# Build-time order of a three-stage attention and gating kernel: VectorE and GpSimd pieces kept apart, TensorE lengths as measured, all choices drawn anew

## The chip, the cores and the metric

One core of one Trainium2 chip runs the kernel. The metric is the device time of one execution in microseconds (us). The profile is one execution, recorded by the hardware profiler. PE is TensorE, DVE is VectorE, ACT is ScalarE, POOL is GpSimd, SP is SyncE, whose queue issues every DMA here.

## The reference

Three stages follow one another for 4 batches (B) of 576 tokens (S), everything in float32:

```python
# 1: attention, 8 heads of 64; tokens in fours (mean), and a band of +-3 tokens
out = repeat(softmax(q_d @ k_d.T / 8) @ v_d, 4) + softmax(band(q @ k.T / 8)) @ v
# 2: 4 experts on x = out (512 channels), each a causal attention of width 64; the 2 best logits of x @ w_gate
x2 = sum over the 2 chosen e of w_e * (softmax(causal(x@wq[e] @ (x@wk[e]).T / 8)) @ (x@wv[e]) @ wo[e])
# 3: gated tail: a causal convolution of 5 taps per channel
y = (sigmoid(conv5(x2)) * (x2 @ w_val)) @ w_out
```

`w_val` and `w_out` arrive as float64 and are rounded to float32 on the chip from their two words. Products of stages 2 and 3 are made of three products of float32r halves (high by high, high by low, low by high), so every operand of them is split once into a high part (ACT) and a low part (a subtraction on DVE or POOL, L499).

## The kernel before, in words

The kernel does not loop over its work in a fixed order. It describes pieces. `@piece(engine, cost, reads, writes)` gives a piece its engine, an estimated length, its buffers and, through `plan.due`, a due time. `Plan.order` is a list scheduler that runs while the kernel is built: whenever an engine is free in its model, it gives that engine the piece due first among those whose inputs are done and for whose buffers there is room. The program is then written in that order, and on the chip each engine runs its list strictly in order, held only by semaphores. Due times are priorities and not clock times.

`PARAMS` holds 336 numbers and names: due times and lengths of the stages (`f`/`fl` attention, `p`/`pl` projections, `e`/`el` experts, `t`/`tl` tail, one per batch; `wq` the weights of q, k, v and gate, `wt`/`wl` those of the tail), how many PSUM banks or buffers a kind may hold (`c_`, `r_`), the engine of single steps (`q_`, `k_`, `v_` the sums of fours at L651 to L685, `n_` the band's normalising at L734, `xl_`, `gl_` the low parts at L499, `w_` the experts' normalising at L1021, `ve_`, `xe_`, `mp_`, `pt_`, `qe_` copies out of PSUM at L489), how many of the 5 taps ACT takes (`cv_`; it multiplies at L1129 and POOL adds at L1133; the other taps are one DVE instruction each at L1138), and in which form a band softmax is done (`a_`).

A batch goes through attention in 4 pairs of heads (scores L745 and L787, maxima L699, their scaling L704, exponentials L709, sums L726 to L730, values L813, sum of both paths L821). Then come projections in 3 products each (L848 to L850), experts by 64 queries (scores again L848 to L850, minima L988, exponentials L997, normalising L1021, transposes L1029, values L1068) and the tail in two halves of 256 and 320 tokens. The result of attention stands in 4 pairs of buffers `xh`, `xl`, which the projections of the same batch free again. A float64 chunk takes DVE steps L526 to L550, ACT steps and three POOL instructions (L558 to L560); it uses the one `v4` buffer and four of the `o` buffers.

The costs that the planner counts with:

```python
def f32r(n):
    return max(0.417 * n, 107) / 1000 + 0.002
def gps(n, k=1):
    return 0.15 * k + 0.0021 * n + 0.102 * (k - 1)
```

It knows nothing of DVE and POOL holding each other up.

Of the kernel before, what the change touches and what calls it, by code (L numbers as in the profile page):

```python
# [21 lines left out]
TINY64 = 2.0 ** -15 * 1.125      # the float whose bits are the upper word of a float64 2^-126  # L22
# [14 lines left out]
    "k_30": "pool", "k_31": "dve", "k_32": "dve", "k_33": "pool", "late": 1.5, "mp_00": "act", "mp_01": "act",  # L37
# [30 lines left out]
    "w_315": "pool", "w_316": "pool", "w_317": "dve", "w_318": "pool", "wl": 88.75, "wl_o": "pool",  # L68
    "wl_out": "dve", "wl_qk": "dve", "wl_vg": "dve", "wq": 71.47, "wt": 39.26, "xe_00": "dve", "xe_01": "dve",
# [7 lines left out]
}  # L77

# [1 line left out]
# The kernel below describes pieces of work: an engine, a rough length, the buffers that are read and  # L80
# written, and when the piece is due. Plan puts them in an order that keeps the engines busy with the
# buffers there are; the program is then written in that order.

class Buf:
    """one use of a slot of a pool"""
# [10 lines left out]
class Piece:  # L96
    def __init__(self, engine, cost, delay, due, fn):
        self.engine, self.cost, self.delay, self.due, self.fn = engine, cost, delay, due, fn
        self.after, self.before, self.bufs, self.needs = set(), [], [], []
        self.ready = 0.0  # L100


class Plan:
    # until the result can be used: by another engine, by the same one
# [15 lines left out]
    def piece(self, engine, cost, reads=(), writes=(), delay=None, after=()):  # L120
        """a piece waits for the writers of what it reads; what it reads and writes, it has to itself"""
        def add(fn):
            p = Piece(engine, cost, self.DELAY[engine] if delay is None else (delay, delay), (self.due, len(self.pieces)), fn)
# [17 lines left out]
            p.after.discard(p)  # L141
            self.pieces.append(p)
            return p
        return add

    def order(self):
        """list scheduling: an engine that is free takes the piece due first of those that can start"""
        free = {k: list(range(len(v))) for k, v in self.pools.items()}
        used = dict.fromkeys(self.caps, 0)
        turn = dict.fromkeys(self.fifo, 0)  # L150
        waiting = {}
        queues = {e: [] for e in self.DELAY}
        for p in self.pieces:
# [24 lines left out]
        while True:  # L178
            for e, queue in queues.items():
# [3 lines left out]
                for i, (_, p) in enumerate(queue):  # L183
                    if room(p):
                        break
# [75 lines left out]
def gps(n, k=1):  # L261
    return 0.15 * k + 0.0021 * n + 0.102 * (k - 1)
# [976 lines left out]
```

## Time and profile before

| | before |
|---|---|
| three runs | 455.19, 456.3, 458.0 us; median 456.3 |
| span of the profiled execution, first to last instruction | 454.2 us |
| busy: PE, DVE, ACT, POOL | 401.4, 383.5, 261.4, 207.6 us |
| moved over the DMA queues | 36.39 MB |

The page gives only the span of the profiled execution; it lies 2.1 us under the median of the runs. A busy PE is one with a product on its way: the records of neighbouring products overlap, so full PE busy time is not PE at its peak.

### The profile page before, as it was taken

To read this page: it belongs to the slowest core of one execution; us is meant where nothing else is said; L and a number is where in the kernel's file an instruction comes from. 1 tells how busy PE (TensorE), PEld (TensorE's weight loads), DVE (VectorE), ACT (ScalarE), POOL (GpSimd) and SP (SyncE) were. 2 spreads that over 40 slices of the span, in tenths; PEclk is the share of its full clock that TensorE was granted. 3 is DMA by queue.
4 is the path that set the end of the run, shared out by engine and by line. 5 is a ranking of instruction groups with operands and counts; after the bars stand their busy time and mean duration, and the time that the engine had idled before them with its cause. 6 is when DMAs were issued, how large, how long until landed. Compare 5 with 4: busy or idle time off the path is not lost.

```text
span 454.2 us, 11162 instructions
## 1 busy us (share of the span) xinstructions
PE 401.4 (88%) x3984; PEld 352.5 (78%) x3984; DVE 383.5 (84%) x1083; ACT 261.4 (58%) x844; POOL 207.6 (46%) x347
## 2 busy tenths in 40 slices
PE   3678688889789578988999899999999999999997
PEld 3467576867568468877977789989887999888996
DVE  6878998698998999669789987697899787979695
ACT  7374655347577666434757754544775534757551
POOL 6355667446663764545454632322342603455100
PEclk9997899999999899999999999999999999999999
DMA  7988665522233111131613040020222000000102
GB/s 179 252 194 222 170 172 134 150 78 75 56 81 100 46 48 48 52 100 30 190 33 107 1 140 13 17 67 30 82 57 57 5 1 0 25 25 2 58 26 79
DMA packets 29078, 36.39 MB, mean 80 GB/s; under 512 B 3424, under 2 KB 18784, under 8 KB 29024
## 3 DMA queue, kind: packets, MB, share of 16 engines
q1 hardware_dynamic: 29024, 35.69, 27.9%
q8 instruction: 31, 0.51, 0.5%
q14 instruction: 23, 0.19, 0.1%
HBM read 30.96 MB, written 4.72 MB: 79 GB/s over the span
## 4 chain that ended last, share of the span: by engine, by line
PE 49%; DVE 33%; DMA 8%; issue 5%; POOL 2%; ACT 1%; SPq 1%; DVEq 0%; POOLq 0%; ACTq 0%
PE ps L848 12%; PE ps L849 10%; PE ps L850 10%; DMA v<-in_vx_dram 5%; DVE row L1138 4%; PE ps L1068 4%; PE ps L1029 3%; PE ps L813 3%; DVE mx L699 2%; DVE pe L1021 2%; DVE mmin L988 2%; PE ps L799 2%; DVE sm L726 2%; PE ps L745 1%; DMA vw<-in_vx_dram 1%
## 5 line engine op out<-in xcount | busy, mean ns | idle before, releaser
L1138 DVE SCALAR_TENSOR_TENSOR row<-row,cw,row 128x256 f32<-128x256 f32 (+1 forms) x96 | 60.2, 638 | 4.0 <-POOL row L1133 2.9
L997 ACT ACTIVATE pe<-ps,mmin 128x64 f32<-128x64 f32 (+4 forms) x80 | 40.0, 502 | 20.4 <-PE ps L1029 8.6
L1029 PE MATMUL ps<-ident,pe 128*128 128x128 f32 x192 | 33.6, 284 | 13.4 <-ACT pe L997 4.6
L1021 POOL TENSOR_SCALAR pe<-pe,es,ew 128x128 f32<-128x128 f32 (+8 forms) x39 | 25.4, 652 | 42.2 <-DVE es L1014 24.7
L709 ACT ACTIVATE p<-ps,mx 128x64 f32<-128x64 f32 (+1 forms) x104 | 34.4, 347 | 16.6 <-DVE mx L704 11.4
L848 PE MATMUL ps<-xh,wqk_h 128*128 128x320 f32 (+1 forms) x128 | 40.2, 314 | 1.4 <-DVE qla L962 0.6
L848 PE MATMUL ps<-gh,wout_h 128*128 128x256 f32 (+1 forms) x128 | 40.4, 316 | 0.0
L988 DVE TENSOR_REDUCE mmin<-ps 128x1 f32<-128x64 f32 (+4 forms) x80 | 35.4, 447 | 5.6 <-PE ps L984 5.0
L849 PE MATMUL ps<-gl,wout_h 128*128 128x256 f32 (+1 forms) x128 | 37.8, 296 | 0.0
L850 PE MATMUL ps<-xh,wqk_l 128*128 128x320 f32 (+1 forms) x128 | 37.8, 295 | 0.0
L849 PE MATMUL ps<-xl,wqk_h 128*128 128x320 f32 (+1 forms) x128 | 37.7, 295 | 0.0
L850 PE MATMUL ps<-gh,wout_l 128*128 128x256 f32 (+1 forms) x128 | 37.7, 295 | 0.0
L787 PE MATMUL ps<-kz,qz 128*64 128x64 f32 x640 | 29.2, 240 | 8.6 <-POOL kz L412 6.5
L1029 PEld LDWEIGHTS ps<-ident,pe 128*128 128x128 f32 x192 | 21.8, 141 | 18.0 <-ACT pe L997 5.0
L1133 POOL TENSOR_TENSOR row<-row,row 128x256 f32<-128x256 f32 (+1 forms) x32 | 26.4, 826 | 20.1 <-ACT row L1129 18.7
L787 PEld LDWEIGHTS ps<-kz,qz 128*64 128x64 f32 x640 | 24.4, 150 | 14.1 <-POOL kz L412 7.0
L1068 PE MATMUL ps<-mpT,vE 128*64 128x256 f32 (+3 forms) x352 | 28.3, 296 | 1.6 <-DVE row L1150 0.9
L499 POOL TENSOR_TENSOR xl<-row,xh 128x348 fp32r<-128x348 f32 (+1 forms) x21 | 17.6, 850 | 26.3 <-ACT xh L495 26.3
L813 PEld LDWEIGHTS ps<-pT,vw 128*64 128x64 f32 x640 | 22.9, 150 | 6.7 <-issue 2.7
L699 DVE TENSOR_REDUCE mx<-ps 128x6 f32<-128x384 f32 (+2 forms) x48 | 24.6, 516 | 3.9 <-PE ps L787 2.7
L813 PE MATMUL ps<-pT,vw 128*64 128x58 f32 (+1 forms) x640 | 26.0, 238 | 2.1 <-ACT p L709 1.3
L499 POOL TENSOR_TENSOR gl<-row,gh 128x320 fp32r<-128x320 f32 (+1 forms) x20 | 18.0, 904 | 20.2 <-ACT gh L495 20.2
(187 smaller groups left out, 1420.2 us busy)
## 6 DMA issues: line engine op xcount, KB each, us to landing
vw<-in_vx_dram SPq DMA_DIRECT2D x32, 160.0 KB
qz<-in_qT_dram SPq DMA_DIRECT2D x32, 144.0 KB
kt<-in_kT_dram SPq DMA_DIRECT2D x16, 288.0 KB
kz<-in_kT_dram SPq DMA_DIRECT2D x32, 144.0 KB
v<-in_vx_dram SPq DMA_DIRECT2D x16, 288.0 KB
out_dram<-o SPq DMA_DIRECT2D x16, 160.0 KB
v<-in_w_val_dram SPq DMA_DIRECT2D x4, 512.0 KB
v<-in_w_out_dram SPq DMA_DIRECT2D x4, 512.0 KB
```

The costliest lines, as they stand in the source:

```text
L499: (nc.vector if eng == "dve" else nc.gpsimd).tensor_sub(lo(), src(), hi().bitcast(F32))
L787: nc.tensor.matmul(s.t[64 * h:64 * h + 64, (w - w0) * 64:(w - w0) * 64 + 64], qb.t[:, h, WQ * w:WQ * w + 64], kz.t[:, h, WQ * w:WQ * w + 6 ...
L813: nc.tensor.matmul(po.t[64 * h:64 * h + 64, q0 - t0:q1 - t0], vw.t[:, w, 64 * h:64 * h + 64], pT.t[:, (w - w0) // 2, 64 * h:64 * h + q1 - ...
L848: nc.tensor.matmul(p, ah, bh, start=first, stop=False)
L849: nc.tensor.matmul(p, ah, bl, start=False, stop=False)
L850: nc.tensor.matmul(p, al, bh, start=False, stop=last)
L988: nc.vector.tensor_reduce(out=m.t[:, a:a + 1], in_=s.t[:, :c1 - c0], op=ALU.min, axis=AX.X)
L997: nc.scalar.activation(pe.t[:, c0:c1], s.t[:, :c1 - c0], AF.Exp, bias=m.t[:, 0:1], scale=-1.0, accum_out=es.t[:, a:a + 1])
L1021: ENG[en].tensor_scalar(pe.t[:, :N], pe.t[:, :N], es.t[:, 0:1], ew.t[:, i % 2, t, pr:pr + 1], op0=ALU.mult, op1=ALU.mult)
L1029: nc.tensor.transpose(pt.t[:, (nf - 1 - j) * P:(nf - j) * P], pe.t[:, j * P:(j + 1) * P], ident)
L1068: nc.tensor.matmul(av.t[64 * e:64 * e + 64, z:n], vE.t[:kr, j, 2 * pr + e, :], pT.t[:kr, e, k0:k0 + (n - z) // 64, :].rearrange("p k q -> ...
L1138: nc.vector.scalar_tensor_tensor(g.t[:, :nn], x2.t[:, k:k + nn], cw.t[:, m, k:k + 1], g.t[:, :nn], op0=ALU.mult, op1=ALU.add)
```

## The change

The planner gets a kind for each piece. DVE and POOL pieces that work in SBUF alone get the kind "port"; TensorE pieces of half-height tiles get "half".

```diff
 class Plan:
-    # until the result can be used: by another engine, by the same one
+
+    PATIENCE, AHEAD, HEAD = 0.1, 4.0, {"dve": 0.13, "pool": 0.05}
...
-                for i, (_, p) in enumerate(queue):
+                other = {"dve": "pool", "pool": "dve"}.get(e)
+                i = None
+                for j, (_, p) in enumerate(queue):
                     if room(p):
-                        break
-                else:
+                        if i is None:
+                            i = j
+
+                        if p.kind != "port" or port[other] <= now + self.PATIENCE:
+                            i = j
+                            break
+                        if p.due[0] > queue[i][1].due[0] + self.AHEAD:
+                            break
+                if i is None:
                     continue
+                p = queue[i][1]
...
+                if p.kind == "port":
+                    cost = max(cost, port[other] - now + cost - min(cost, self.HEAD[e]))
+                    port[e] = now + cost
                 if e == "pe":
-                    # the array runs at half its rate after a beat with much idling
+                    if p.kind != groups:
+                        cost += 0.09 if p.kind else 0.14
+                        groups = p.kind
...
-def f32r(n):                     # one float32r product
-    return max(0.417 * n, 107) / 1000 + 0.002
...
+def f32r(n):
+    return max(0.459 * n, 112) / 1000
...
-    return 0.15 * k + 0.0021 * n + 0.102 * (k - 1)
+    return 0.19 * k + 0.0021 * n + 0.08 * (k - 1)
```

A port piece is passed over while a port piece of the other engine runs on for more than 0.1 us, if another piece that can start is due at most 4 us later; otherwise it is placed anyway, with the wait added to its length. A few more lengths change by some hundredths of a microsecond.

No instruction's arithmetic changes, nor the number of TensorE products. `PARAMS` is drawn anew: of the choices of engine 9 of 16 change for `v_`, 7 of 16 for `k_`, 5 of 16 for `q_`, 17 of 32 for `n_`, 16 of 32 for `xl_`, 34 of 72 for `w_`, 4 of 8 for `gl_`. The count of band parts with a scaled maximum (`a_` 1) goes from 11 to 18 of 32. Taps on ACT: `cv_00` 2 to 4, `cv_01` 2 to 1, `cv_10` 2 to 1, `cv_11` 2 to 4, `cv_20` 3 to 4, `cv_21` 3 to 1, `cv_30` 1 to 2, `cv_31` stays 1. To ACT go `ve_0`, `ve_1`, `mp_20`, `mp_31`, `xe_01`, `xe_20`, `pt_3`, `qe_31`; to DVE go `pt_1`, `qe_10`, `qe_20`, `qe_21`; `wl_qk` goes from DVE to POOL. Due times: `wq` 71.47 to 251.21, `wt` 39.26 to 27.09, `f1` 34.43 to 31.69 with `fl1` 21.4 to 87.16, `p0` 60.17 to 103.9, `e2` 196.82 to 68.9 with `el2` 42.86 to 204.57, and all others.

## Rows read from the trace of the kernel before

**Rows 1.** The page, busy us, share of the span and instructions of each engine.
```profile
PE 401.4 (88%) x3984; PEld 352.5 (78%) x3984; DVE 383.5 (84%) x1083; ACT 261.4 (58%) x844; POOL 207.6 (46%) x347
```
**Rows 2.** Stretches: us, busy PE, PEld, DVE, ACT, POOL, granted clock, DMA share, GB/s.
```profile
0.00:40.00 40.00, 26.19 (x276) 21.72 (x278) 31.02 (x86) 23.98 (x81) 20.71 (x48) 0.92 0.86 205
40.00:180.00 140.00, 112.37 (x1193) 92.42 (x1190) 129.07 (x349) 86.06 (x289) 85.24 (x119) 0.97 0.36 104
180.00:260.00 80.00, 72.93 (x736) 64.95 (x737) 66.75 (x191) 46.94 (x153) 40.12 (x64) 1.00 0.25 73
260.00:440.00 180.00, 179.04 (x1715) 163.07 (x1712) 148.06 (x441) 101.05 (x316) 61.50 (x118) 1.00 0.12 37
440.00:454.20 14.20, 10.87 (x77) 10.33 (x75) 8.64 (x20) 3.37 (x8) 0.00 (x0) 0.98 0.21 77
```
**Rows 3.** The page, the chain that ended last, share of the span by engine.
```profile
PE 49%; DVE 33%; DMA 8%; issue 5%; POOL 2%; ACT 1%; SPq 1%; DVEq 0%; POOLq 0%; ACTq 0%
```
**Rows 4.** Waits of PE between 260 and 440 us, the longest: us, times, longest.
```profile
PE ps L848 <- DVE qla L962: 0.6, 1, 0.6
```
**Rows 5.** Waits of all engines between 40 and 180 us: us, times, longest.
```profile
ACT p L709 <- DVE mx L704: 9.8, 7, 2.3
...
PE ps L1029 <- ACT pe L997: 4.6, 1, 4.6
```
**Rows 6.** Groups of DVE between 40 and 180 us: busy us, mean ns, idle before.
```profile
L1138 DVE SCALAR_TENSOR_TENSOR row<-row,cw,row 128x256 f32<-128x256 f32 x12 | 10.6, 882 | 0.1
...
L1021 DVE TENSOR_SCALAR pe<-pe,es,ew 128x384 f32<-128x384 f32 (+6 forms) x9 | 6.7, 748 | 0.1
L726 DVE TENSOR_SCALAR sm<-sm 128x4 f32<-128x4 f32 (+2 forms) x22 | 6.4, 298 | 0.1
...
L704 DVE TENSOR_SCALAR mx<-mx 112x3 f32<-112x3 f32 (+2 forms) x12 | 5.9, 493 | 0.1
```
**Rows 7.** The same lines over the span: ns min/median/max, first and last start us.
```profile
L1138 DVE SCALAR_TENSOR_TENSOR row<-row,cw,row x96: 461/541/1545, 145.2 to 444.9; 128x256 f32<-128x256 f32 x48, 128x320 f32<-128x320 f32 x48
...
L1021 DVE TENSOR_SCALAR pe<-pe,es,ew x33: 308/500/1517, 128.4 to 410.4; 128x192 f32<-128x192 f32 x5, 128x576 f32<-128x576 f32 x5, 128x64 f32<-128x64 f32 x4, 128x320 f32<-128x320 f32 x4
...
L726 DVE TENSOR_SCALAR sm<-sm x48: 139/169/1245, 14.3 to 354.5; 128x6 f32<-128x6 f32 x16, 112x3 f32<-112x3 f32 x16, 128x4 f32<-128x4 f32 x16
...
L704 DVE TENSOR_SCALAR mx<-mx x27: 124/169/1236, 9.5 to 345.8; 112x3 f32<-112x3 f32 x16, 128x6 f32<-128x6 f32 x6, 128x4 f32<-128x4 f32 x5
```
**Rows 8.** Groups of POOL between 40 and 180 us: the three costliest.
```profile
L560 POOL TENSOR_TENSOR o<-o,o 128x512 f32<-128x512 f32 (+1 forms) x11 | 10.6, 967 | 0.9
L558 POOL TENSOR_TENSOR o<-o,o 128x512 f32<-128x512 f32 (+1 forms) x11 | 10.2, 929 | 16.7 <-ACT o L554 12.8 <-DVE qlb L962 3.3 <-ACT ah L495 0.4
L559 POOL TENSOR_TENSOR o<-o,o 128x512 f32<-128x512 f32 (+1 forms) x11 | 10.0, 909 | 0.9
```
**Rows 9.** Groups of DVE by shape, over the span: copies out of PSUM, low parts.
```profile
L489 DVE COPY vE<-ps 128x256 f32<-128x256 f32 x12 | 4.9, 412 | 3.5 <-PE ps L850 3.5
...
L489 DVE COPY row<-ps 128x320 f32<-128x320 f32 x8 | 3.9, 486 | 2.9 <-PE ps L850 2.0 <-ACT xh L495 0.6
...
L499 DVE TENSOR_TENSOR wqk_l<-o,wqk_h 128x512 fp32r<-128x512 f32 x4 | 3.1, 766 | 0.0
```
**Rows 10.** Lines 499 and 489 over the span: ns min/median/max, first and last start.
```profile
L499 DVE TENSOR_TENSOR gl<-row,gh x12: 401/422/627, 360.8 to 447.0; 128x256 fp32r<-128x256 f32 x8, 128x320 fp32r<-128x320 f32 x4
...
L489 DVE COPY pT<-ps x8: 411/484/558, 324.4 to 356.7; 128x384 f32<-128x384 f32 x4, 128x256 f32<-128x256 f32 x4
```
**Rows 11.** The chain that ended last, before 40 us: start us, us, what.
```profile
16.59 4.95 DMA o<-in_wvg_dram
```
**Rows 12.** Line 848, the first products of a projection: ns min/median/max, starts.
```profile
L848 PE MATMUL ps<-wvg_h,xh x80: 277/284/390, 61.6 to 366.0; 128*128 128x260 f32 x64, 128*64 128x260 f32 x16
```

More of the change, by code (lines that the diff above doesn't have):

```diff
@@ L25 @@
 PARAMS = {
[11 rows of a table removed]
-    "k_30": "pool", "k_31": "dve", "k_32": "dve", "k_33": "pool", "late": 1.5, "mp_00": "act", "mp_01": "act",
[30 rows of a table removed]
-    "w_315": "pool", "w_316": "pool", "w_317": "dve", "w_318": "pool", "wl": 88.75, "wl_o": "pool",
-    "wl_out": "dve", "wl_qk": "dve", "wl_vg": "dve", "wq": 71.47, "wt": 39.26, "xe_00": "dve", "xe_01": "dve",
[7 rows of a table removed]
[4 rows of a table added]
+    7, "c_mo": 2, "c_ms": 2, "c_mt": 4, "c_o": 2, "c_s": 4, "c_t": 4, "c_w": 5, "cv_00": 4, "cv_01": 1,
[4 rows of a table added]
+    "pool", "gl_31": "dve", "k_00": "dve", "k_01": "pool", "k_02": "pool", "k_03": "dve", "k_10": "pool",
+    "k_11": "dve", "k_12": "dve", "k_13": "dve", "k_20": "pool", "k_21": "pool", "k_22": "dve", "k_23":
+    "pool", "k_30": "pool", "k_31": "dve", "k_32": "pool", "k_33": "dve", "late": 47.15, "mp_00": "act",
[10 rows of a table added]
+    "act", "pt_1": "dve", "pt_2": "act", "pt_3": "act", "q_00": "dve", "q_01": "dve", "q_02": "dve",
+    "q_03": "dve", "q_10": "dve", "q_11": "dve", "q_12": "pool", "q_13": "pool", "q_20": "pool", "q_21":
+    "pool", "q_22": "pool", "q_23": "pool", "q_30": "pool", "q_31": "dve", "q_32": "pool", "q_33": "pool",
[4 rows of a table added]
+    "pool", "v_20": "dve", "v_21": "pool", "v_22": "pool", "v_23": "dve", "v_30": "dve", "v_31": "pool",
[13 rows of a table added]
+    "wl_o": "pool", "wl_out": "dve", "wl_qk": "pool", "wl_vg": "dve", "wq": 251.21, "wt": 27.09, "xe_00":
+    "dve", "xe_01": "act", "xe_10": "act", "xe_11": "dve", "xe_20": "act", "xe_21": "act", "xe_30": "act",
+    "xe_31": "act", "xl_000": "pool", "xl_001": "pool", "xl_010": "dve", "xl_011": "dve", "xl_020":
+    "pool", "xl_021": "dve", "xl_030": "pool", "xl_031": "dve", "xl_100": "pool", "xl_101": "dve",
+    "xl_110": "pool", "xl_111": "pool", "xl_120": "dve", "xl_121": "dve", "xl_130": "pool", "xl_131":
+    "dve", "xl_200": "dve", "xl_201": "pool", "xl_210": "pool", "xl_211": "pool", "xl_220": "dve",
+    "xl_221": "pool", "xl_230": "pool", "xl_231": "dve", "xl_300": "dve", "xl_301": "dve", "xl_310":
+    "dve", "xl_311": "pool", "xl_320": "dve", "xl_321": "dve", "xl_330": "dve", "xl_331": "pool",
 }
@@ L96, with __init__ @@
 class Piece:
-    def __init__(self, engine, cost, delay, due, fn):
-        self.engine, self.cost, self.delay, self.due, self.fn = engine, cost, delay, due, fn
+    def __init__(self, engine, cost, delay, due, fn, kind):
+        self.engine, self.cost, self.delay, self.due, self.fn, self.kind = engine, cost, delay, due, fn, kind
         self.after, self.before, self.bufs, self.needs = set(), [], [], []
@@ L118, in buf, with piece @@
         return b
-    def piece(self, engine, cost, reads=(), writes=(), delay=None, after=()):
+    def piece(self, engine, cost, reads=(), writes=(), delay=None, after=(), kind=None):
         def add(fn):
-            p = Piece(engine, cost, self.DELAY[engine] if delay is None else (delay, delay), (self.due, len(self.pieces)), fn)
+            k = ("port" if engine == "pool" else "") if kind is None else kind
+            p = Piece(engine, cost, self.DELAY[engine] if delay is None else (delay, delay), (self.due, len(self.pieces)), fn, k)
             rd = [(b, None) if isinstance(b, Buf) else (b[0], b[1] if isinstance(b[1], tuple) else (b[1],)) for b in reads]
@@ L165, in order @@
         beat, active = 4096 / 1200, {}
+        port = {"dve": 0.0, "pool": 0.0}
+        groups = ""
         def room(p):
@@ L261, in gps, with port @@
 def gps(n, k=1):
-    return 0.15 * k + 0.0021 * n + 0.102 * (k - 1)
+    return 0.19 * k + 0.0021 * n + 0.08 * (k - 1)
+def port(eng):
+    return "port" if eng in ("dve", "pool") else None
 @with_exitstack
@@ L414, in tile_local_attention__then__moe__then__gated_conv @@
         for t in pools["qz"]:
-            @piece("dve", 0.68, after=[eye])
+            @piece("dve", 0.68, after=[eye], kind="port")
             def rows(t=t, o=o, h=h):
@@ L486, in copy @@
     def copy(eng, n, out, src, reads, writes):
-        @piece(eng, cost(eng, n, reads[0]), reads, writes)
+        @piece(eng, cost(eng, n, reads[0]), reads, writes, kind=port(eng) if reads[0].pool != "ps" else None)
         def _():
@@ L495, in _ @@
             nc.scalar.copy(hi(), src())
-        @piece(eng, vec(n) if eng == "dve" else gps(n), [read, wh], [wl])
+        @piece(eng, vec(n) if eng == "dve" else gps(n), [read, wh], [wl], kind=port(eng) if read.pool != "ps" else None)
         def _():
@@ L521, in _ @@
             nc.sync.dma_start(out=raw.t[:, :2 * n].bitcast(I32), in_=rows.bitcast(I32))
-        @piece("dve", vec(n / 2, 1), [raw], [a0, a1, ss])
+        @piece("dve", vec(n / 2, 1), [raw], [a0, a1, ss], kind="port")
         def _():
             nc.vector.tensor_scalar(part(0), words(1), 0x08000000, 3, op0=ALU.bitwise_xor, op1=ALU.logical_shift_left)
-        @piece("dve", vec(n / 2, 1), [a0], [a0])
+        @piece("dve", vec(n / 2, 1), [a0], [a0], kind="port")
         def _():
@@ L538, in _ @@
             nc.scalar.activation(ss.t[:, :n], words(1).bitcast(F32), AF.Sign)
-        @piece("dve", vec(n), [a0, a1], [f])
+        @piece("dve", vec(n), [a0, a1], [f], kind="port")
         def _():
@@ L544, in _ @@
                                            op0=ALU.is_ge, op1=ALU.mult)
-        @piece("dve", vec(n, 2), [raw, f, a0, a1], [a0, a1])
+        @piece("dve", vec(n, 2), [raw, f, a0, a1], [a0, a1], kind="port")
         def _():
@@ L571, in weights_qkv @@
             f = chunk(wqk, c, 512)
-            @piece("dve", vec(128), [f], [f])
+            @piece("dve", vec(128), [f], [f], kind="port")
             def _(f=f):
@@ L593, in weights_tail @@
             f = chunk(convT, c, TAPS)
-            @piece("dve", 0.1, [f], [(cw, c)])
+            @piece("dve", 0.1, [f], [(cw, c)], kind="port")
             def _(c=c, f=f):
@@ L646, in load_pair @@
             r = slice(64 * h, 64 * h + 64)
-            @piece(en, cost(en, 2 * SD), [qb], [(t1, h), (qd, "own")])
+            @piece(en, cost(en, 2 * SD) - 0.13 * (en == "pool"), [qb], [(t1, h), (qd, "own")], kind=port(en))
             def _(r=r, h=h, eng=eq):
@@ L654, in load_pair @@
             r = slice(64 * h, 64 * h + 64)
-            @piece(en, cost(en, SD) + 0.06 * (en == "pool"), [(t1, h)], [qd], after=[blocks])
+            @piece(en, cost(en, SD) - 0.06 * (en == "pool"), [(t1, h)], [qd], after=[blocks], kind=port(en))
             def _(r=r, h=h, eng=eq):
@@ L662, in load_pair @@
         ek = ENG[en]
-        @piece(en, cost(en, 2 * SD), [kt], [t2, (kd, "own")])
+        @piece(en, cost(en, 2 * SD) - 0.13 * (en == "pool"), [kt], [t2, (kd, "own")], kind=port(en))
         def _(eng=ek):
@@ L667, in _ @@
             eng.tensor_add(t2.t[:, :2 * SD].rearrange("p (j r) -> p j r", r=2), kv[:, :, 0:2], kv[:, :, 2:4])
-        @piece(en, cost(en, SD) + 0.06 * (en == "pool"), [t2], [kd])
+        @piece(en, cost(en, SD) - 0.06 * (en == "pool"), [t2], [kd], kind=port(en))
         def _(eng=ek):
@@ L675, in load_pair @@
         ev = ENG[en]
-        @piece(en, cost(en, 4 * P), [v4], [v4])
+        @piece(en, cost(en, 4 * P), [v4], [v4], kind=port(en))
         def _(eng=ev):
@@ L680, in _ @@
             eng.tensor_add(v[:, :, 0:2], v[:, :, 0:2], v[:, :, 2:4])
-        @piece(en, cost(en, 2 * P), [v4], [vd])
+        @piece(en, cost(en, 2 * P), [v4], [vd], kind=port(en))
         def _(eng=ev):
@@ L701, in softmax @@
         if each:
-            @piece("dve", vec(g), [mx], [mx])
+            @piece("dve", vec(g), [mx], [mx], kind="port")
             def _():
@@ L722, in _ @@
                 nc.vector.tensor_reduce(out=sm.t[:n, :g], in_=pv(), op=ALU.add, axis=AX.X)
-        @piece("dve", vec(g), [sm], [sm])
+        @piece("dve", vec(g), [sm], [sm], kind="port")
         def _():
@@ L730, in _ @@
             nc.vector.reciprocal(sm.t[:n, :g], sm.t[:n, :g])
-        @piece(norm, cost(norm, g * w), [p, sm], [p])
+        @piece(norm, cost(norm, g * w) - 0.15 * (norm == "pool"), [p, sm], [p], kind=port(norm))
         def _():
@@ L762, in down_path @@
         po = bank("o")
-        @piece("pe", 0.56, [vd, pdT], [po])
+        @piece("pe", 0.55, [vd, pdT], [po], kind="half")
         def _():
@@ L780, in band_scores @@
         s = bank("s")
-        @piece("pe", 0.155 * g, [qb, kz], [s], after=queries + masks)
+        @piece("pe", 0.1415 * g, [qb, kz], [s], after=queries + masks, kind="half")
         def _():
@@ L794, in band_values @@
         pT, pt = buf("pT"), bank("t")
-        @piece("pe", 0.055 * g, [p], [pt], after=down)
+        @piece("pe", 0.062 * g, [p], [pt], after=down)
         def _():
@@ L805, in band_values @@
         n = t1 - t0
-        @piece("pe", 0.153 * g, [vw, pT, od], [po], after=blanks)
+        @piece("pe", 0.141 * g, [vw, pT, od], [po], after=blanks, kind="half")
         def _():
@@ L855, in gates @@
         sh = [P, NTOK, E, E]
-        @piece("dve", 1.66, [L], [ge, gw, gm])
+        @piece("dve", 1.66, [L], [ge, gw, gm], kind="port")
         def _():
@@ L874, in _ @@
             nc.scalar.activation(gw.t[:, 0], gw.t[:, 0], AF.Exp)
-        @piece("dve", 0.95, [gw, gm], [gw, gm])
+        @piece("dve", 0.95, [gw, gm], [gw, gm], kind="port")
         def _():
@@ L885, in gates @@
         pw, ew = bank("d"), buf("ew")
-        @piece("pe", 0.28, [gw], [pw])
+        @piece("pe", 0.28, [gw], [pw], kind="half")
         def _():
@@ L976, in expert_rows @@
             s = bank("ms")
-            @piece("pe", (0.285 if c1 <= P else 3 * f32r(c1 - c0)) + (0.025 if c1 == N else 0.0),
+            @piece("pe", 3 * f32r(max(c1, P) - c0) + (0.08 if c1 == N else 0.0),
                    [(qh, mine), (ql, mine), (kh, half), (kl, half)], [s])
@@ L990, in expert_rows @@
         if len(parts) == 2:
-            @piece("dve", 0.08, [m], [m])
+            @piece("dve", 0.08, [m], [m], kind="port")
             def _():
@@ L999, in expert_rows @@
         if i % 2 == 0 and nb * P <= S:
-            @piece("pool", 0.09, [(m, 0)], [(pe, N)])
+            @piece("pool", 0.11, [(m, 0)], [(pe, N)], kind="free")
             def _():
@@ L1017, in expert_rows @@
         en = PARAMS["w_%d%d%d" % (b, pr, i)]
-        @piece(en, 0.19 + 0.00053 * N if en == "dve" else 0.33 + 0.00084 * N, [pe, es, ew], [pe])
+        @piece(en, 0.19 + 0.00053 * N if en == "dve" else 0.33 + 0.00084 * N, [pe, es, ew], [pe], kind=port(en))
         def _():
@@ L1060, in experts @@
                 blocks = [(j, 0 if j < T else 64 * lead) for j in range(T + 1)]
-                @piece("pe", sum(0.05 + 0.00163 * (n - z) for _, z in blocks), [pT, (vE, tuple(range(T + 1)))], [av])
+                @piece("pe", sum(0.05 + 0.00163 * (n - z) for _, z in blocks), [pT, (vE, tuple(range(T + 1)))], [av], kind="half")
                 def _(pT=pT, vE=vE, av=av, blocks=blocks, n=n, T=T, w=w, lead=lead, pr=pr):
@@ L1101, in gated @@
         product(w_o, p)
-        @piece("pool", 0.09, [p, old] if old else [p], [(x2, 0)])
+        @piece("pool", 0.15 if old else 0.06, [p, old] if old else [p], [(x2, 0)], kind=None if old else "free")
         def _():
@@ L1135, in gated @@
         for k in range(form, TAPS):
-            @piece("dve", vec(nn) + 0.063, [x2, g, (cw, (m,))], [g])
+            @piece("dve", vec(nn) + 0.063, [x2, g, (cw, (m,))], [g], kind="port")
             def _(k=k):
```

83 rows, old and new, of the table PARAMS are left out of this document.

## The prediction

> **What bounds the kernel now.** I read the page's busy times first [rows 1]. PE is busy 401.4 us of a span of 454.2 and DVE 383.5, so either could be the bound, and the shares alone do not say where. The stretches decide it [rows 2]. Between 260 and 440 us PE is busy 179.0 of 180 us, and its longest single wait is 0.6 us [rows 4]: here only PE counts, and whatever DVE, ACT or POOL gain is given back as idle time. Between 40 and 180 us it is the other way round: DVE is busy 129.1 of 140 us, PE 112.4. Between 180 and 260 us neither is full (PE 72.9, DVE 66.8 of 80). Ahead of 40 us the DMA engines are busy 0.86 of the time and PE works 26.2 of 40 us. PE thus idles 13.8 + 27.6 + 7.1 + 1.0 + 3.3 = 52.8 us, 48.5 of them ahead of 260 us. A better order can save that idle time and little else; PE's work is the same afterwards. The chain that ended last says the same: PE 49%, DVE 33%, DMA 8% [rows 3].
>
> Why is DVE full from 40 to 180 us? Part of its busy time is waiting. The scaling of 3 to 6 numbers per row (L704, L726) has a median of 169 ns over the span, but 1236 and 1245 ns at worst, and a tap (L1138) goes from a median of 541 to 1545 ns [rows 7]. No work on so few elements takes a microsecond; what lasts about so long is a POOL instruction (L558 to L560 average 0.91 to 0.97 us, five-column ones included) [rows 8]. I read this as DVE held until POOL's instruction ends. It reaches PE: ACT waits 9.8 us in all for L704 in this stretch, and PE 4.6 us at once for an exponential [rows 5].
>
> **The parts of the change and their costs.** The sum is made against the span of 454.2 us; the median of the runs lies 2.1 us above it, and I add that at the end.
>
> *Port pieces kept apart.* What is lost to the holding, by line, is the count times (mean of the stretch less the median of the span) [rows 6, 7]. L1138: 12 x (882 - 541) = 4.1 us. L1021: 9 x (748 - 500) = 2.2. L726: 22 x (298 - 169) = 2.8. L704: 12 x (493 - 169) = 3.9. Sum 13.0 us of the 29.6 us that these four lines are busy. The other DVE lines of the stretch, 129.1 - 29.6 = 99.5 us, also have SBUF-only work that loses, so 13.0 is a floor of the loss; if they lose as much again, it is 26. Not all of it returns. Where the planner puts a DVE piece that reads PSUM beside a POOL piece, DVE's wait goes; where it finds none, DVE idles instead of waiting, and one late DMA shifts the engines against each other so that pairs meet again. I set these against each other and take 10 us for 40 to 180 us, the value near the floor, since that is counted from rows. For 180 to 260 us I take 3: POOL is busy 40.1 of 80 us there, a little less densely than before (85.2 of 140), the stretch is about half as long, and DVE is not full, so that half of the saving is idle time anyway. Ends: 0 (all waits return as idle time) and 30 (all 26, and 4). After 260 us: 0, hidden by PE.
>
> The Trainium skill ("SBUF — State Buffer", section "Who interferes with whom") states that DVE and GpSimd share one pair of ports as an exclusive lock, held for a whole instruction by whichever starts first, and that the other blocks fully. The rows on L704 and L726 agree. The rule speaks against the change in one point: order changes who waits, and the time on the pair stays the same; by it the sum of this part alone would be anything from 0 up, by how much PSUM work fits beside. That is the first rival below.
>
> *Engine choices.* Only what falls on DVE ahead of 260 us counts. Weights: four low parts of 512 columns go to POOL, 4 x 0.766 = -3.1 us [rows 9]. Batch 0: five copies to ACT, 5 x 0.412 = -2.1; four copies to ACT, 4 x 0.486 = -1.9 [rows 9]; eight taps fewer and four more, -4 x 0.541 = -2.2 [rows 7]; four low parts more, 4 x 0.422 = +1.7 [rows 10]. Together -4.5. Batch 1: copies -2.1 [rows 9], taps -4 x 0.541 = -2.2 [rows 7], low parts +1.7, eight copies of L489 for `pt_1` 8 x 0.484 = +3.9 [rows 10], four for `qe_10` at 0.412 to 0.486, some +1.8 [rows 9]; together +3.1. The sums of fours, the normalising and the experts' scaling go both ways by a few instructions each; I put them at 0, between -4 and +4. Sum -4.5, of which I take -4. ACT takes on the copies and taps: it is busy 86.1 of 140 us [rows 2], which is the cover; without it the copies would cost what they save. In batches 2 and 3 DVE sheds more (`mp_20`, `mp_31`, `pt_3`), worth nothing where PE is full.
>
> *TensorE lengths and other costs.* They change only where the planner thinks PE is free. 0, between -8 (denser PE in 260 to 440 us, where the records overlap and may hide small gaps) and +6 (buffers freed later than planned).
>
> *New due times.* The q, k, v and gate weights move from 71.47 to 251.21, behind the tail's weights and behind batch 1's attention. Their eight DMAs leave the head of SP's queue to the pair loads, and the chain holds 4.95 us of waiting for such a chunk at 16.6 us [rows 11]; but the queue is full there either way, so the pair loads inherit most of that wait. 0, between -5 and, if the weights come too late, the second rival.
>
> Sum: -10 - 3 - 4 = -17; 454.2 - 17 = 437.2, and with 2.1 **439 us**. PE idle ahead of 260 us would fall from 48.5 to some 31 us, and the PE-bound stretch would start and end earlier by as much. What is late next is PE itself.
>
> **The rivals.** About 1% is what a measurement of this kernel can tell from no change: 451.7 to 460.9 us.
>
> *The pair is the bound.* If the waits come back as idle time, only the engine choices are left: 454.2 - 4 + 2.1 = 452, and with pairs that meet again about 454. For it: DVE 129.1 and POOL 85.2 of 140 us leave little room beside each other [rows 2]. Against it: 99.5 of DVE's 129.1 us lie outside the four lines that lose most, and much of that reads PSUM (maxima, minima, copies), which the planner can put beside POOL. 18%.
>
> *Late weights: slower.* The first projection product of batch 0 now starts at 61.6 us [rows 12]. Batch 1's attention cannot finish a pair until that projection has freed `xh` and `xl`. If the tail's float64 chunks go first, with their chain through POOL (10.6 + 10.2 + 10.0 = 30.8 us [rows 8]) and the four `o` buffers that the other weights need too, the projection is held by up to those 30.8 us. Less the gain of 17, that is +14: 454.2 + 14 + 2.1 = 470; with half of the delay, 455. It decides from a first projection product later than about 61.6 + 17 = 79 us. For it: the due time itself. Against it: a chunk of 260 or 512 columns needs one `o` buffer, a float64 chunk four and `v4`, so the small ones slip in wherever SP and a buffer are free. 16%.
>
> *PE filled from 40 us on.* If nearly all idle time of PE between 40 and 440 us goes, 27.6 + 7.1 + 1.0 = 35.7 us, the time is 454.2 - 35.7 + 2.1 = 421. For it: with DVE's waits gone and everything drawn anew on truer lengths, DVE may stop being the bound. Against it: the stages of a batch depend on each other, and PE waits in 40 to 180 us for ACT and DVE chains, not for one engine. 16%.
>
> That the change does nothing can be excluded: the order and the engine choices are written out differently.
>
> **How the numbers follow.** The forecast has 50%. Its own range goes from 426 (all 26 us of the stretch for 10, less a little) to 450 (2 us from each part and the bad end of the lengths), all of it faster by over 1%. Faster: 50 + 16 and a tenth of the 18 of the first rival, 68%. Within 1%: the rest of the first rival, less a little that goes to the slower side, 15%. Slower: 16 and that little, 17%. For 8 in 10 the range must reach into the third rival and most of the second: below 419 I leave out 8%, above 461 some 12%.
>
> **What would show it.** The scaling at L704 and L726 should have means near 0.2 us and few instances over 0.6; a tap's mean should fall from 0.64 us towards 0.55. DVE's busy time should fall by more than the 17 us that the path wins, since the late batches shed DVE work as well. PE's idle time ahead of 260 us should be near 31 us, and PE should be full in the last 180 us as before. It would be wrong if the means fall and PE's idle time stays (first rival), if the first projection product comes after 79 us (second), or if PE idles under 20 us in all (third).

## The result and the profile after

The changed kernel takes 443.9 us (median) against 455.9 us for the kernel before in the same series, a ratio of 0.972 with a 95% interval of 0.967 to 0.978. The forecast was 439 us in a range of 419 to 461. Ratios and intervals, here and below, leave out a few executions that were slower at a lower clock; medians are of all.

The page's busy times and its chain, after (busy us, share of the span, instructions; then shares of the chain):

```profile
span 444.2 us, 11206 instructions
...
PE 400.0 (90%) x3984; PEld 354.6 (80%) x3984; DVE 352.5 (79%) x1055; ACT 279.0 (63%) x945; POOL 203.3 (46%) x340
...
PE 54%; DVE 21%; DMA 10%; ACT 5%; POOL 5%; issue 3%; SPq 1%; POOLq 0%; DVEq 0%; ACTq 0%
```

Against [rows 1, 3], DVE lost 31 us of busy time and went from 33% to 21% of the chain; PE's work stayed. The same stretches as [rows 2], after (busy PE, PEld, DVE, ACT, POOL; granted clock, DMA share, GB/s):

```profile
0.00:40.00 40.00, 22.68 (x256) 18.66 (x256) 29.77 (x81) 26.12 (x102) 16.50 (x43) 0.87 0.83 202
40.00:180.00 140.00, 126.96 (x1321) 108.73 (x1321) 118.00 (x367) 90.64 (x314) 89.11 (x123) 0.97 0.37 102
180.00:260.00 80.00, 71.58 (x757) 62.99 (x759) 68.55 (x205) 48.29 (x169) 41.64 (x63) 0.94 0.35 98
260.00:440.00 180.00, 177.85 (x1649) 163.57 (x1648) 136.17 (x406) 113.37 (x362) 56.10 (x113) 1.00 0.10 31
```

PE's idle time, before and after: ahead of 40 us 13.8 and 17.3, from 40 to 180 us 27.6 and 13.0, to 260 us 7.1 and 8.4, to 440 us 1.0 and 2.2, then 3.3 twice. The whole gain lies between 40 and 180 us (14.6 us, with 1321 products done there and not 1193); the other stretches give back 6 us (3.5 of them ahead of 40 us, which is not shown to be a loss: see "New due times" below). Idle time falls by 8.6 us in all and PE's busy time by 1.4, which is the 10.0 us between the two profiled spans; the medians lie 12.0 us apart.

The four lines of [rows 6], after, between 40 and 180 us (L1164 is L1138 of before, L1047 is L1021, L752 is L726, L730 is L704; count, busy us, mean ns, idle before):

```profile
L752 DVE TENSOR_SCALAR sm<-sm 112x3 f32<-112x3 f32 (+2 forms) x20 | 6.4, 326 | 0.1
L1047 DVE TENSOR_SCALAR pe<-pe,es,ew 128x64 f32<-128x64 f32 (+4 forms) x7 | 4.2, 606 | 0.0
L730 DVE TENSOR_SCALAR mx<-mx 112x3 f32<-112x3 f32 (+2 forms) x12 | 3.8, 324 | 0.0
...
L1164 DVE SCALAR_TENSOR_TENSOR row<-row,cw,row 128x256 f32<-128x256 f32 x4 | 1.9, 477 | 0.0
```

Beside [rows 6]: taps run undisturbed at 477 ns (882 before), but there are 4 of them in the stretch and not 12. The other eight did not leave through the order: all are of batch 0's first half, where `cv_00` gave them to ACT. L730 fell from 493 to 324 ns; L752 rose from 298 to 326. Against a median of 0.17 us (shown below), a mean of 0.33 us on three to six numbers is still half waiting. The trace shows one meeting of a DVE and a POOL piece, in order of time (start us, us):

```profile
175.99 1.28 POOL L584 TENSOR_TENSOR o<-o,o 128x512 f32<-128x512 f32 x1 [2.71 <-DVE row L1176]
...
176.04 1.27 DVE L905 TENSOR_TENSOR gw<-gw 128x20 f32<-128x20 f32 x1
```

An elementwise product of DVE on 20 columns starts 50 ns after POOL's and ends 40 ns after it. So semaphores are not all that holds an engine here. The Trainium skill ("SBUF — State Buffer", section "Who interferes with whom") states that a DVE instruction with two SBUF inputs contends with a GpSimd instruction that reads SBUF, and calls the port pair that the two engines share an exclusive lock. These rows agree. The order is written to keep such pairs apart where another piece is due soon enough, and on the chip some still meet.

### The profile page after: what moved, and what is told of

The parts are those of the page before. It is cut to its first block, busy times and chain, and to the rows that moved or that the text cites. A ratio compares the mean times of both kernels' runs of the same rounds, so it can differ in the third digit from the quotient of the medians.

```text
span 444.2 us, 11206 instructions
## 1 busy us (share of the span) xinstructions
PE 400.0 (90%) x3984; PEld 354.6 (80%) x3984; DVE 352.5 (79%) x1055; ACT 279.0 (63%) x945; POOL 203.3 (46%) x340
## 4 chain that ended last, share of the span: by engine, by line
PE 54%; DVE 21%; DMA 10%; ACT 5%; POOL 5%; issue 3%; SPq 1%; POOLq 0%; DVEq 0%; ACTq 0%
PE ps L874 13%; PE ps L876 11%; PE ps L875 11%; DMA v<-in_vx_dram 8%; PE ps L1094 5%; PE ps L1055 4%; PE ps L839 2%; PE ps L813 2%; DVE p L760 2%; DVE mx L725 2%; DMA out_dram<-o 2%; PE ps L771 1%; PE ps L612 1%; PE ps L780 1%; DVE row L1164 1%
## 5 line engine op out<-in xcount | busy, mean ns | idle before, releaser
L1047 POOL TENSOR_SCALAR pe<-pe,es,ew 128x384 f32<-128x384 f32 (+8 forms) x37 | 25.7, 696 | 62.4 <-DVE es L1040 22.7
L735 ACT ACTIVATE p<-ps,mx 128x64 f32<-128x64 f32 (+1 forms) x140 | 45.3, 344 | 13.2 <-DVE mx L730 11.1
L1164 DVE SCALAR_TENSOR_TENSOR row<-row,cw,row 128x320 f32<-128x320 f32 (+1 forms) x88 | 47.9, 556 | 4.5 <-ACT row L1147 3.0
L874 PE MATMUL ps<-gh,wout_h 128*128 128x256 f32 (+1 forms) x128 | 42.4, 331 | 0.1
L1159 POOL TENSOR_TENSOR row<-row,row 128x256 f32<-128x256 f32 (+1 forms) x40 | 32.4, 811 | 21.0 <-ACT row L1155 17.1
L813 PEld LDWEIGHTS ps<-kz,qz 128*64 128x64 f32 x640 | 26.4, 159 | 14.8 <-POOL cmask L472 6.0
L813 PE MATMUL ps<-kz,qz 128*64 128x64 f32 x640 | 30.5, 248 | 8.2 <-DMA kz<-in_kT_dram 6.9
L515 ACT COPY mpT<-ps 128x512 f32<-128x512 f32 (+3 forms) x54 | 23.7, 447 | 14.8 <-PE ps L1055 13.6
L735 ACT ACTIVATION_READ_ACCUMULATOR p<-ps,mx 128x1 f32 (+1 forms) x140 | 29.9, 214 | 0.0
L839 PEld LDWEIGHTS ps<-pT,vw 128*64 128x64 f32 x640 | 21.8, 143 | 7.2 <-ACT pT L515 4.4
L725 DVE TENSOR_REDUCE mx<-ps 128x6 f32<-128x384 f32 (+2 forms) x48 | 24.7, 519 | 2.7 <-PE ps L813 1.9
```

The lines of the kernel that those rows point to most:

```text
L725: nc.vector.tensor_reduce(out=mx.t[:n, :g], in_=sv(), op=ALU.max, axis=AX.X)
L735: nc.scalar.activation(pv()[:, i], sv()[:, i], AF.Exp, scale=scale, bias=mx.t[:n, i:i + 1], accum_out=sm.t[:n, i:i + 1])
L813: nc.tensor.matmul(s.t[64 * h:64 * h + 64, (w - w0) * 64:(w - w0) * 64 + 64], qb.t[:, h, WQ * w:WQ * w + 64], kz.t[:, h, WQ * w:WQ * w + 6 ...
L839: nc.tensor.matmul(po.t[64 * h:64 * h + 64, q0 - t0:q1 - t0], vw.t[:, w, 64 * h:64 * h + 64], pT.t[:, (w - w0) // 2, 64 * h:64 * h + q1 - ...
L874: nc.tensor.matmul(p, ah, bh, start=first, stop=False)
L1164: nc.vector.scalar_tensor_tensor(g.t[:, :nn], x2.t[:, k:k + nn], cw.t[:, m, k:k + 1], g.t[:, :nn], op0=ALU.mult, op1=ALU.add)
```

## The experiments

Three theories stand against each other. Theory 1: keeping the port pieces apart won the time. Theory 2: the new choices won it, under any planner. Theory 3, formed after the first four runs: PARAMS are the best of many draws under exactly one planner, and any other order loses by the luck of the draw. Ratios below are to the kernel before in the same series, with their 95% intervals.

**Planner and choices crossed.**

```diff
 e1: kernel before
-PARAMS = {"a_000": 1, "a_001": 0, ... of the kernel before
+PARAMS = {"a_000": 1, "a_001": 0, ... of the changed kernel
 e2: changed kernel
-PARAMS of the changed kernel
+PARAMS of the kernel before
```

e1. 

> The planner and the lengths of the kernel before, with the new PARAMS. If keeping the port pieces apart won the time (theory 1), that is lost here: 455 us or more, DVE busy near 375 us, the scaling at L704 and L726 with means near 0.33 us as before. If the newly drawn choices won it, whatever planner orders them (theory 2), about 444 us.

Measured: 457.8 us, 1.003 (1.000 to 1.007). DVE is busy 362.2 us, 21.3 less than before; the time did not move. That refutes theory 2 as put, for any planner, and the simple form of "DVE is the bound": in this order 21 us less of DVE work bring nothing.

e2. 

> The new planner with its lengths, and the PARAMS of the kernel before. Theory 1: most of the gain is here, 444 to 449 us. Theory 2: no gain, 456 us or more, since due times that were drawn for one planner mean another order under the other.

Measured: 478.1 us, 1.051 (1.044 to 1.057). DVE is busy 370.3 us, 13.2 less than before, with the same choices of engine: the new planner does keep DVE from waiting. But PE idles 479.6 - 411.4 = 68.2 us and not 52.8. Theory 1, as put, falls.

**Parts of the planner taken out.**

```diff
 e3: changed kernel
-                        if p.kind != "port" or port[other] <= now + self.PATIENCE:
-                            i = j
-                            break
-                        if p.due[0] > queue[i][1].due[0] + self.AHEAD:
-                            break
+                            break
...
-                if p.kind == "port":
-                    cost = max(cost, port[other] - now + cost - min(cost, self.HEAD[e]))
-                    port[e] = now + cost
 e4: changed kernel
-    return max(0.459 * n, 112) / 1000
+    return max(0.417 * n, 107) / 1000 + 0.002
...
-                    if p.kind != groups:
-                        cost += 0.09 if p.kind else 0.14
-                        groups = p.kind
```

e3. 

> The changed kernel whose planner neither passes over port pieces nor counts their waits; its TensorE lengths stay. Theory 1: slower by the 12 us won, 454 to 458 us, DVE busy up by 20 us or more to 370 us. Theory 2, or a gain from truer TensorE lengths: 444 to 448 us.

Measured: 477.7 us, 1.048 (1.042 to 1.054): 34 us slower than with the rule, nearly three times all that the change won. DVE is busy 366.6 us, 14.1 more than with the rule.

e4. 

> The changed kernel with the port rule, but the old length of a float32r product and no cost for a change between groups of products. Theory 1: 443 to 447 us. If the truer TensorE lengths matter as much as the rule: 450 us or more.

Measured: 467.3 us, 1.028 (1.022 to 1.034). Each part alone seems worth far more than both together brought; that is no sum of parts, and it led to theory 3.

**Numbers moved that mean nothing.**

```diff
 e6: changed kernel
-    DELAY = {"pe": (0.23, 0.0),
+    DELAY = {"pe": (0.24, 0.0),
 e7: kernel before
-"act": (0.22, 0.212),
+"act": (0.23, 0.212),
```

e6. 

> The changed kernel with one number of the planner moved by nothing that matters: the delay after a TensorE piece 0.24 and not 0.23 us. Theory 3 (PARAMS are the best of many draws under exactly this planner, and any other order is worse by the luck of the draw): 455 to 470 us. If the losses of the runs without the port rule and without the new TensorE lengths were the worth of these: within 3 us of the changed kernel, 441 to 447 us.

Measured: 466.1 us, 1.020 (1.014 to 1.027).

e7. 

> The kernel before with the delay after an ACT piece 0.23 and not 0.22 us. Theory 3: 465 to 485 us, as its PARAMS too are the best of many draws. Rival: 453 to 459 us.

Measured: 479.2 us, 1.046 (1.036 to 1.055).

Ten nanoseconds in one assumed delay cost 22 us in the changed kernel and 23 us in the kernel before. Both came out as theory 3 expects: an order for which PARAMS were not drawn loses. The stretches, first of e6, then of e7 (columns as above):

```profile
40.00:180.00 140.00, 121.43 (x1182) 101.02 (x1182) 109.85 (x326) 83.17 (x283) 84.23 (x115) 0.90 0.34 92
```

```profile
40.00:180.00 140.00, 109.98 (x1115) 90.55 (x1112) 125.65 (x342) 85.14 (x284) 86.19 (x118) 0.90 0.36 103
...
260.00:440.00 180.00, 169.07 (x1622) 152.56 (x1618) 142.78 (x424) 95.84 (x312) 66.46 (x116) 0.97 0.14 39
```

In e6 DVE is less busy from 40 to 180 us than in the changed kernel (109.9 and 118.0), and PE still idles 18.6 us there and not 13.0, with 139 products fewer. No engine is full there. The 5.6 us of idle time are too little for 139 products; the granted clock, 0.90 and not 0.97, is lower too. Over the span PE's busy time is 410.7 us in e6 and 400.0 in the changed kernel, for the same 3984 products, so about half of the 20.6 us between these spans is not idle time of PE but longer busy time. The same is seen in e2 (10.0 us more busy time than before) and e3 (13.5 us more than with the rule).

So the losses of e3 and e4 cannot be read as the worth of the rule or of the lengths: an empty nudge costs as much as e4. Nor can the times of e1 and e2 be read as the worth of the choices or of the planner, since each of them is another order too. DVE's busy time is steadier than the time: the nudges moved it by 4.5 us (e6) and 1.1 us (e7), while the planner took 13.2 us off it in e2 and the rule's removal put 14.1 us on it in e3. That the rule takes waits off DVE is shown by this; what that is worth in time is not.

**What POOL's hold costs with the order kept.** Shorter POOL instructions leave every engine's list as it was.

```diff
 e5: kernel before; e12: changed kernel
-            nc.gpsimd.tensor_mul(a0.t[:, :n], a0.t[:, :n], a1.t[:, :n])
-            nc.gpsimd.tensor_add(f.t[:, :n], f.t[:, :n], a0.t[:, :n])
-            nc.gpsimd.tensor_mul(f.t[:, :n], f.t[:, :n], ss.t[:, :n])
+            nc.gpsimd.tensor_mul(a0.t[:, :5], a0.t[:, :5], a1.t[:, :5])
+            nc.gpsimd.tensor_add(f.t[:, :5], f.t[:, :5], a0.t[:, :5])
+            nc.gpsimd.tensor_mul(f.t[:, :5], f.t[:, :5], ss.t[:, :5])
```

e5. 

> The kernel before, in its order, with POOL's three steps per float64 chunk (L558 to L560) on 5 columns and not 512: 24 instructions of 1.3 us shrink to 0.2 us, some 26 us of POOL less between 57 and 190 us. It leaves out the lower word's share of w_val and w_out on the other columns. If POOL's hold on DVE sets the time of that stretch (theory 1): L704 and L726 at means near 0.2 us there, and 445 to 449 us. If the order sets it and the held time is slack: 452 to 456 us.

Measured: 446.3 us, 0.976 (0.969 to 0.984), 10.3 us less than the kernel before in its series. The stretch and DVE's groups in it:

```profile
40.00:180.00 140.00, 123.37 (x1264) 103.47 (x1264) 119.15 (x364) 88.90 (x296) 63.86 (x124) 0.94 0.39 107
```

```profile
L1138 DVE SCALAR_TENSOR_TENSOR row<-row,cw,row 128x256 f32<-128x256 f32 x12 | 5.7, 473 | 0.1
L1021 DVE TENSOR_SCALAR pe<-pe,es,ew 128x384 f32<-128x384 f32 (+6 forms) x9 | 4.6, 514 | 0.1
L726 DVE TENSOR_SCALAR sm<-sm 128x4 f32<-128x4 f32 (+2 forms) x22 | 4.4, 209 | 0.1
L704 DVE TENSOR_SCALAR mx<-mx 112x3 f32<-112x3 f32 (+2 forms) x12 | 2.6, 216 | 0.1
```

The same 55 instructions as in [rows 6], in the same order, take 17.3 us and not 29.6. The 12.3 us that they lose are close to the 13.0 that the prediction counted by medians, and PE is busy 11.0 us more in the stretch. The wait for POOL was real, it lay on the path there, and it was worth some 10 us. One reservation: POOL's own chain for the float64 weights also gets shorter, and the run does not part the two.

e12. 

> The changed kernel in its order, with POOL's three steps per float64 chunk (now L584 to L586) on 5 columns and not 512, as was done to the kernel before; it leaves out the lower word's share of w_val and w_out on the other columns. If the new order really keeps DVE clear of POOL: 1 to 3 us won, 441 to 443 us. If the holds remain and the gain came from the order of the stages: 434 to 438 us, as much as the 10 us that the kernel before won.

Measured: 439.4 us, 0.963 (0.959 to 0.967), so 4.5 us less than the changed kernel. It lies between the two expectations. In the stretch L752 goes from 326 to 298 ns, L730 from 324 to 221, L1047 from 606 to 372. Between 40 and 260 us PE idles 17.0 us and not 21.4. The new order and the new choices together have taken about 10.3 - 4.5 = 5.8 us of what POOL's float64 steps cost, and left the rest. By the intervals each of the two differences is good to some 3 us and 5.8 to some 5.

**PARAMS drawn afresh with and without the rule.** Both planners got the same start and the same effort; e9 and e10 have the edit of e3.

```diff
 e8, e9, e10: one mixture of both PARAMS as the start, then
-PARAMS of the changed kernel
+PARAMS of the shortest plan of some 16,000 random changes
```

e8. 

> The new planner with PARAMS drawn afresh: start from a half-and-half mixture of the old and the new PARAMS, one chain of some 16,000 random changes, the shortest plan kept. Theory 1 (the port rule is worth the gain once PARAMS are drawn for it): 443 to 452 us, 8 us or more ahead of the two draws without the rule. Theory 3 alone (any planner does as well, if PARAMS are drawn for it): level with those within 4 us.

e9. 

> The new planner without the port rule (it neither passes over port pieces nor counts their waits; new TensorE lengths), PARAMS drawn from the same mixture with as many random changes. Theory 1: 453 to 462 us, L730 and L752 at means near 0.33 us, DVE busy 370 us or more. Theory 3 alone: the same time as the draw with the rule, within 4 us.

e10. 

> A second draw without the port rule, other random changes from the same start, to show how far two draws lie apart. Theory 1: 453 to 462 us. Theory 3 alone: level with the draw with the rule within 4 us.

Measured, as ratios: 0.989 (0.984 to 0.994) with the rule, 1.002 (0.998 to 1.005) and 1.026 (1.020 to 1.031) without; the medians are 453.1, 457.8 and 467.5 us. The draw with the rule is ahead by 4.7 and 14.4 us, but the two draws without it lie 9.7 us apart, and there is only one with it. DVE is busy 363.2 us with the rule, 374.7 and 376.1 without. That the rule pays once PARAMS are drawn for it is what these three point to; they do not settle it, since the luck of the draw alone is as large as the difference. For the same reason the expectation of theory 3 alone, all three level within 4 us, fails without refuting it. The draw of the changed kernel (0.972) is 1.7% ahead of e8, which has the same planner; e8 is 1.3% ahead of e9.

**A version to beat both.**

```diff
 e11: changed kernel
-"e2": 68.9, "p3": 297.99, "c_mo": 2, "wq": 251.21,
+"e2": 106.32, "p3": 264.47, "c_mo": 6, "wq": 193.5,
...
```

e11. 

> The changed kernel's planner untouched; PARAMS drawn on from its own, but each draw is judged by playing its fixed order with transfers that share some 200 GB/s and with the port wait, not by the planner's own length, in which every transfer lands 1.5 us after its issue. If what the changed kernel lacks is in the order against late transfers: 434 to 441 us. If 444 us is what this planner can give: 442 to 448 us.

Measured: a ratio of 0.979 (0.974 to 0.985), level with the changed kernel's 0.972 within the intervals. Judging draws with shared transfers did not find a better order.

## Why the prediction was right, and where it was not

**The bound, stretch by stretch: right.** PE fills 260 to 440 us before and after (179.0 and 177.9 of 180), and nothing was won there. The time came out of the stretches ahead of that, as said. The size was less: the terms foretold 10 + 3 + 4 = 17 us between 40 and 260 us, and PE's idle time there fell from 34.7 to 21.4, by 13.3. Ahead of 260 us PE idles 38.7 us and not the 31 that the prediction named as its sign.

**"Port pieces kept apart", 13 us: right mechanism, term too large.** The medians over the span, after, and the longest:

```profile
L752 DVE TENSOR_SCALAR sm<-sm x48: 122/168/1229, 13.3 to 339.0; 128x6 f32<-128x6 f32 x16, 128x4 f32<-128x4 f32 x16, 112x3 f32<-112x3 f32 x16
...
L730 DVE TENSOR_SCALAR mx<-mx x34: 129/167/1221, 11.2 to 333.7; 112x3 f32<-112x3 f32 x16, 128x6 f32<-128x6 f32 x10, 128x4 f32<-128x4 f32 x8
```

By the prediction's own count (L1047's median is 450 ns) the four lines now lose 12 x (324 - 167) + 20 x (326 - 168) + 7 x (606 - 450) = 6.1 us in the stretch, none of it on the taps, against 13.0 before, so 6.9 us came back. Of these, 8 x (882 - 541) = 2.7 us went with the eight taps that `cv_00` gave to ACT, a choice and not the rule; 4.2 us are left for the order. e5 and e12 give 5.8 for order and choices together. Both are below the 10 us of the term. The signs named for it came half true: the taps' mean fell from 638 to 556 ns as said, but L730 (295 over the span) and L752 (241) did not come near 0.2 us, and their longest are still 1221 and 1229 ns. The 3 us for 180 to 260 us did not come at all: idle time rose by 1.3. One wait, from 177.7 to 183.7 us, is 6.0 us long, and the hold is part of it:

```profile
PE ps L917 <- ACT p L735: 6.0, 1, 6.0
...
177.55 1.09 DVE L907 TENSOR_SCALAR gm<-gm 128x5 f32<-128x5 f32 x1
...
178.90 1.09 DVE L909 TENSOR_TENSOR gw<-gw,gm 128x20 f32<-128x20 f32 x1
```

From 176.04 to 179.99 us DVE does L905 (shown above), L907 and L909 in 1.27, 1.09 and 1.09 us, each beside one of the three float64 steps of POOL. Only then, at 179.91 us, does it take up the next maxima (L725), whose scores were done by 176.6 us. Six exponentials in a row on ACT, each with its own accumulator read, follow from 181.74 to 183.5 us, and the next product of PE starts at 183.68; `a_200` is among the parts that went to this form. In e12, where POOL's steps are short, the three DVE instructions take 0.18, 0.17 and 0.58 us and the same wait is 3.5 us: 2.5 us of the 6.0 go with the hold, at a place where the new order did not avoid it. The wait costs more than its idle time. The page gives PE's granted clock in 40 equal slices of the span, one digit each, in tenths; the 17th digit, 5, is the slice from 177.7 to 188.8 us:

```profile
PEclk9968999999899999599999999999999999999999
```

From 184.6 to 189.3 us the granted clock is at its lower level (0.50, 1.2 GHz) and products of 256 columns start 214 ns apart; from 189.7 us on it is 1.00 and they start 118 to 120 ns apart. For the 21 products in between that is some 2 us, an estimate from these two paces, and the profile counts it as busy time of PE.

**"Engine choices", 4 us: the direction right, its worth not shown.** They cost DVE 21.3 us less over the span (e1 against before). In the old planner's order that brought 1.003, but that order is a new one too. By its own rule, only what falls ahead of 260 us, the prediction also counted too much: the taps of batch 1's second half run between 260 and 298 us before, so what `cv_11` and `gl_11` change there does not count, and the sum is -4.5 - 3.1 + 5.8 = -1.8 us and not -4.5. (Of the choices listed above it is `qe_30` that went to ACT, not `qe_31`; `oe_2` and `oe_3` changed as well. All are of batches 2 and 3.)

**"TensorE lengths", 0: open.** e4 lost 23 us without them, and e6 lost 22 without anything.

**"New due times", 0: no loss shown.** The second rival did not come: the first projection product starts at 62.6 us (61.6 before, limit 79).

```profile
L874 PE MATMUL ps<-wvg_h,xh x80: 278/284/389, 62.6 to 360.0; 128*128 128x260 f32 x64, 128*64 128x260 f32 x16
```

Ahead of 40 us PE idles 17.3 us and not 13.8. But it idles 18.0 us there in e5 too:

```profile
0.00:40.00 40.00, 22.03 (x268) 18.26 (x268) 30.48 (x84) 23.65 (x81) 19.25 (x48) 0.87 0.88 201
```

e5 has the order of the kernel before, and its first shortened step starts only at 71.7 us. So 3.5 us are no more than two executions of one order differ by, and no loss can be laid to the due times.

**What the prediction lacked.** It took the order as given and summed changes to it. e6 and e7 show that the order alone is worth 22 us, more than every term of the sum and more than the whole result. It also put PE's work at the same afterwards. That held here (401.4 and 400.0 us busy), but e2, e3 and e6 show that a worse order makes PE's busy time longer too. The sum came within 5 us of the measured time (17 us foretold, 12.0 measured), but that is in part luck: of the 13.3 us that PE's idle time fell by between 40 and 260 us, only some 4 to 6 can be laid to POOL's hold. The rest, and which of draw, choices and lengths brought it, stays open, since no run here changes one of these and keeps the order.

## What to carry to other kernels

Where a program writes its order from a planner with tuned numbers, time any single change to it only beside a change that should do nothing: if that costs as much, the order is being measured. To price a suspected hold, keep every engine's list and shorten the holder (e5): that gave 10.3 us where counting instances over their median had given 13.0 (it shortens the holder's own chain as well). A wait removed from an engine that looks full is worth time only in the stretches where that engine's list is what the critical engine waits for.

## What was not expected of the hardware

In these two traces a DVE `tensor_scalar` on one column per row never waits for POOL, while the same operation on three to six columns does. Before and after, the 64 instances of the sum's guard on one column (L1010, then L1036):

```profile
L1010 DVE TENSOR_SCALAR es<-es x64: 126/142/155, 115.4 to 410.0; 128x1 f32<-128x1 f32 x64
```

```profile
L1036 DVE TENSOR_SCALAR es<-es x64: 119/145/156, 93.7 to 391.6; 128x1 f32<-128x1 f32 x64
```

The longest is 156 ns, against 1245 ns before [rows 7] and 1229 ns after (L752 above) on three to six columns. They do meet: of the 128 on one column, at least 25 start while an elementwise instruction of POOL has more than 0.2 us to go, and they take 0.13 to 0.16 us all the same. Of those on three to six columns (L704, L726, L730, L752), 29 are seen to start so; 27 of them end 0.01 to 0.12 us after POOL's, and the other two, both beside POOL's `tensor_scalar` (L1021, L1047), take 0.17 us. The planner marks the three to six columns as "port" and the one column not, and the traces bear it out.
